# QK-norm attention and SwiGLU block on one core: what the first dummy matmuls read, when the first raw weights are loaded, and a new plan for the weight conversions

## The chip, the cores and the metric

The kernel runs on one core of a Trainium2 chip. The metric is the device time in microseconds (us) of one execution. Each engine works through its own instruction stream in order: PE (TensorE, matmuls), ACT (ScalarE), DVE (VectorE), POOL (GpSimd) and SP (SyncE, here the queue that issues nearly all DMAs). The streams are held together by semaphores only.

## The reference: what is computed

```
q_n, k_n = rmsnorm(q) * g_q, rmsnorm(k) * g_k        # q, k, v: 8 x 12 x 448 x 64
attn     = softmax(q_n @ k_n^T / sqrt(64)) @ v
x        = attn, heads side by side                   # 3584 x 768
out      = (silu(x @ w_gate) * (x @ w_val)) @ w_out   # 768 -> 1536 -> 768
```

`rmsnorm` divides every row of 64 by the root of its mean square plus 1e-6. The weights reach the kernel as 64-bit floats; all else is float32.

## The kernel before, in words

`fast` (line 494) does the work. Two heads of one batch are a pair; there are 48 pairs. Two batches (12 pairs) make a block of the feed-forward part. The kernel first runs attention for pairs 0 to 11, which I call the early phase. Then it alternates: the up products of a block (gate and value, L1467), and the down products of that block (L1650) with the next twelve pairs of attention laid between them. The products use a fast 3x3 matrix scheme with 15 small products. It needs sums and differences ("sides") of weight blocks and of activation blocks, so each raw weight piece is first converted.

**Attention of one pair** (`attention`, L734). SP loads q and k (L759). ACT squares them (L801; POOL does it for pairs 2 and 3, L799) and DVE sums the squares (in two halves for pair 0, L820; in one go for the others, L829). `inverse_root` (L698) then takes the reciprocal root: logarithm and exponential on ACT (L706, L707) and three short steps on DVE (L712 to L714). DVE (pair 0) or POOL (the others) multiplies q and k by the root (L876). PE turns them (L903), DVE drains the turned keys (L911) and ACT the turned queries (L913). After that come the scores (L965), the exponentials on ACT (L980), the row sums (L1074), the weighted values (L1043), and a division on DVE (L1118 to L1144).

**Dummy matmuls** (`warm`, L1739). Their results are used nowhere; they keep PE busy while it has nothing else. Four run at the start on a tile `more` of zeros. Two follow pair 0's root (L716, L717), one of them on the root itself; one has pair 1's keys as its moving operand (L803); one follows pair 0's transposes (L905).

**Converting weights** (`convert`, L1250). There are 24 raw pieces: 16 of the up weights (four for each of four groups g) and 8 of the down weights. Each takes five DMAs on SP (L1266, L1268), two passes on ACT (L1276, L1280), six or nine short steps on DVE (L1297, L1303, L1309), twelve steps on POOL (L1330, L1333) and one store to DRAM on SP (L1358). A piece lies meanwhile in a "place", a stretch of a tile that something else needs later: XS (inside `xs`), HS, ES, GT (inside `gt`), SPARE, PAIRS (inside `work`, which also holds q, k and what is made of them). Piece n+1 of a place waits for the store of piece n. The up products load converted weights on SP (L1422), three loads for each group; a group's loads follow all four of its stores.

**What sets the order.** Nothing is scheduled by hand, and nothing at run time. A planner (`Order`, L365) gets every step with an engine, an estimated duration, a due time (`when`), a rank that moves the due time forward, and the steps that it must follow. It simulates the engines and emits the instructions in the order so found, which becomes fixed for each engine. So a changed due time, rank or dependency can move steps on every queue. The due times of the conversions come from `starts`, `spans` and `counts` (L1766 to L1768): the first seven are planned 9.9 us apart from 7.0 us on; their places come from `turns` (L1765). `MORE` (L668) shifts the planned time of everything from the end of the first block's up products on.

Of the kernel before, what the change touches and what calls it, by code (L numbers as in the profile page):

```python
# [360 lines left out]
def transfer(rows, size):  # L361
    return rows * (6.64 + 0.045 * min(size, 4096)) / 16000.0
# [131 lines left out]
def fast(  # L494
# [41 lines left out]
    nc = tc.nc  # L536
# [3 lines left out]
    P = 128  # L540
# [124 lines left out]
    PRODUCT = 1.504  # L665
    UP, DOWN, BOTH = 30 * NG * PRODUCT, 90.7, 170.0

    MORE = 4.4  # L668

    def block_start(n):  # L670
        return FIRST + n * (UP + BOTH) + MORE * (n > 0)
# [26 lines left out]
    def inverse_root(m, sums, of, when, rank=0.0, tiny=0.0):  # L698


        def estimate():
            ss = of()
            rr = take("rr", m, [P, 2 * NC])[0 : ss.shape[0], 0 : ss.shape[1]]
            tiles["rr", m] = rr
            bias = little[0 : ss.shape[0]] if tiny else 0.0
            nc.scalar.activation(rr, ss, AF.Ln, bias=bias, scale=GAIN**-2)  # L706
            nc.scalar.activation(rr, rr, AF.Exp, scale=-0.5)  # L707

        def improve():
            ss, rr = of(), tiles["rr", m]  # L710
            times = nc.vector.scalar_tensor_tensor
            times(ss, ss, tiny, rr, op0=ALU.add, op1=ALU.mult)  # L712
            times(ss, ss, -0.5 * GAIN**-2, rr, op0=ALU.mult, op1=ALU.mult)
            times(rr, ss, 1.5, rr, op0=ALU.add, op1=ALU.mult)  # L714
            if m == 0:
                warm(rr)  # L716
                warm(more[:, 0])  # L717

        first = order.add(
            "ACT", 0.48, when, estimate, after=[sums], uses=[("ss", m)], takes=[("rr", m)],  # L720
            mode="logarithms", rank=rank,
        )
        return order.add(
            "DVE", 0.63, when + 1.0, improve, after=[first], uses=[("ss", m), ("rr", m)],
            rank=rank, port=True,
        )
# [7 lines left out]
    def attention(m):  # L734
# [19 lines left out]
        def load(x, src):  # L754
            def emit():
                if natural:
                    to = take("qk", (m, x), [R, 2, NJ * D])
                    rows = src[b][2 * c : 2 * c + 2].rearrange("h (p j) d -> p h (j d)", j=NJ)
                    queue.dma_start(to, rows)  # L759
                    return  # L760
                to = take("qk", (m, x), [P, NC, C])
                for g in range(P // C):
                    rows = src[b, 2 * c + g // 2][:, ts(g % 2, C)]
                    queue.dma_start(to[ts(g, C)], rows.rearrange("(c i) f -> i c f", i=C))  # L764


            both = m == 0 and src is k and not natural
            queue = nc.scalar if both else nc.sync
            return add(
                "ACT" if both else "SP", 0.5 if natural else 1.4 if both else 2.4, ready - 28.0, emit, takes=[("qk", (m, x))],  # L770
                moves=[transfer(2 * R, 4 * NJ * D)] if natural else [transfer(S, 4 * C)] * (P // C), early=25.0,
                after=[staged.get(PAIRS)],
            )

        natural = m in NATURAL
        loaded = [load(x, src) for x, src in enumerate((q, k))]

        def load_values():
            x = take("v", m, [P, NJ, 2, D])
# [12 lines left out]
        def square(x):  # L792
            if x == 0:
                take("t", m, [R, 2, 2 * NJ * D] if natural else [P, 2, NC, C])
            of = tiles["qk", (m, x)]
            if natural:
                of = of.rearrange("p h f -> p (h f)")
            if m in SQUARED:
                nc.gpsimd.tensor_tensor(out=tiles["t", m][:, x], in0=of, in1=of, op=ALU.mult)  # L799
            else:  # L800
                nc.scalar.activation(tiles["t", m][:, x], of, AF.Square)  # L801
            if m == 1 and x == 1:
                warm(of[:, 0:S])  # L803

        squares = []
        for x in range(2):
            squares.append(
                add(
                    "POOL" if m in SQUARED else "ACT", 1.04 if m in SQUARED else 0.63 if natural else 0.58,
                    ready - 18.0, lambda x=x: square(x), port=m in SQUARED,  # L810
                    after=[loaded[x], *squares], uses=[("qk", (m, x))] + [("t", m)] * x,
                    takes=[("t", m)] * (1 - x),
                )
            )
# [35 lines left out]
            )  # L850

        sums = None
        for x in range(2 if m == 0 else 0):
            sums = add(
                "DVE", 0.65, ready - 17.0, lambda x=x: summed_half(x), after=[squares[x], sums],
                uses=[("t", m)] + [("ss", m)] * x, takes=[("ss", m)] * (1 - x),
            )
        sums = sums or add(
            "DVE", 1.45 if natural else 1.08, ready - 17.0, summed,
            after=[*squares, clusters.get("turned") if m == 1 else None], uses=[("t", m)], takes=[("ss", m)]  # L860
        )
        if not natural:
            sums = add("ACT", 0.88, ready - 16.0, swap, after=[sums], uses=[("ss", m)])
# [34 lines left out]
        def turn(x):  # L898
            if x:
                take("st", (m, "turned"), [P, 2, TB])  # L900
            turned = tiles["st", (m, "turned")][:, x]
            for j in range(NJ):
                nc.tensor.transpose(turned[:, ts(j, R)], tiles["t", m][:, x, ts(j, P)], ident[0:R, 0:R])  # L903
            if m == 0 and x == 0:
                warm(more[:, 0, 0:Q])  # L905

        def drain(x):
            turned = tiles["st", (m, "turned")][:, x, 0:S].rearrange("p (j r) -> p r j", j=NJ)
# [258 lines left out]
        )  # L1167
        if b % 2 and c % 3 == 2:
            if early:
                first_sides.append((c // 3, when + 6.0, when + 6.0 - 16.0))  # L1170
            else:
                sides(b // 2, c // 3, when + 6.0)

# [11 lines left out]
    def sides(n, c, when, soon=None):  # L1185
# [7 lines left out]
        for i, one, two, op in (  # L1193
# [15 lines left out]
            if n == 0:  # L1209
# [4 lines left out]
                order.add(  # L1214
                    "DVE", 0.62, soon if soon is not None and i in (6, 8, 1, 10, 13, 9) else when,
                    lambda to=x[i], one=x[one], two=x[two], op=op: combined(to, one, two, op),
                    after=[*done[one], *done[two], *free], port=True, rank=55.0 * (n == 0),
                )
            ]
        for i in SLOT:  # L1220
# [28 lines left out]

    def convert(key, src, sums, to, when, place, by_bank):  # L1250

        rank = 0.0 if by_bank else 5.0

        def add(*what, **more):
            return order.add(*what, **dict(rank=rank, **more))
# [6 lines left out]
        def load():  # L1262
# [5 lines left out]
                nc.sync.dma_start(to[:, i], src(k, n))  # L1268

        loaded = add(  # L1270
            "SP", 2.5, when - 12.0, load, after=[staged.get(place), *wait], moves=[transfer(P * n, 8 * P) for n in (2, 2, 3, 1, 1)], early=3.0
        )
        bits = dst.bitcast(U32)
        one = add(
# [158 lines left out]
    def block(n):  # L1433
# [127 lines left out]
        def up_load(g, piece):  # L1561
# [3 lines left out]
                lambda: load_sides(key, up_sides[g], UP_ORDER[5 * piece :][:5], UP_SUMS),  # L1565
                after=[*last_load, *(weights["up", 4 * g + i] for i in range(4))], takes=[key],
                moves=[transfer(4 * P, 4 * P * i) for i in groups(UP_ORDER[5 * piece :][:5], UP_SUMS)],
                early=8.0,
            )
            last_load[:] = [load]  # L1570
            return key, load
# [164 lines left out]

    def warm(of):  # L1739
        rows, n = of.shape  # L1740
        nc.tensor.matmul(banks[0][:, 0:n], more[0:rows, 0, 0:P], of, start=True, stop=True)

    nc.vector.memset(more[:, 0], 0.0)
    for _ in range(4):
        warm(more[:, 0])
    load_tables()
    order.mode["ACT"] = "logarithms"
    for t, x in ((gq2, g_q), (gk2, g_k)):
# [13 lines left out]
    for m in range(EARLY):  # L1762
        attention(m)
    first = [(up_weights, i) for i in range(4 * NG)] + [(down_weights, i) for i in range(2 * NG)]
    turns = [(XS[0], XS[1], HS, SPARE, GT[1], GT[0], HS, SPARE, GT[1],), (SPARE, PAIRS, HS, GT[2], ES,), (PAIRS, SPARE, ES, HS,)]  # L1765
    starts = [LEAD - 3.4, FIRST - 40.1, FIRST + 78.2]  # L1766
    spans = [9.9, 8.3, 9.9]
    counts = [7, 9, 8]  # L1768
    todo = iter(first)
    for n in range(3):  # L1770
# [77 lines left out]
```

## Time and profile before

| | us |
|---|---|
| runs without profile | 1456.33, 1459.54, 1459.80 (median 1459.54) |
| the profiled execution: its own time | 1457.2 |
| its span, first to last instruction | 1455.4 |
| PE busy in the span | 1424.7 |
| first score matmul (L965) starts | 15.20 |
| first exponential of a pair (L980) starts | 16.66 |
| first up product (L1467) starts | 125.14 |

The table is read from the left end of the run: PE has work in almost every microsecond from the first score matmul on, so the time is mostly PE's fixed work, plus the head (until the scores of pair 0 can start), plus short waits, plus the last stores. Times inside the run are counted from the start of the span.

### The profile page before, as it was taken

What the parts mean: (1) busy time and instruction counts of PE and PEld (TensorE: products, weight loads), DVE (VectorE), ACT (ScalarE), POOL (GpSimd) and SP (SyncE); (2) the same over time, 40 slices, a digit from 0 to 9 for tenths busy, and PEclk for the clock granted to TensorE, in tenths of its full rate; (3) what the DMA queues carried; (4) which work ended last, traced back from release to release, by engine and by line L of the source; (5) the groups of instructions that cost most, each with busy time, mean ns of one, the idle gap of its engine ahead of it and who ended that gap; (6) DMA issues with size and microseconds to landing.
All of it is one profiled execution on the core that took longest, in us unless ns stands there. A gap on an engine that the chain in (4) does not pass through costs nothing.

```text
span 1455.4 us, 19339 instructions
## 1 busy us (share of the span) xinstructions
PE 1424.7 (98%) x6736; PEld 689.5 (47%) x6736; DVE 880.6 (61%) x1484; ACT 601.8 (41%) x1210; POOL 401.0 (28%) x476
## 2 busy tenths in 40 slices
PE   8999999999999999999999999999999999999997
PEld 4454455534444555544444455544444445555553
DVE  5888877888766334546877642356676644442533
ACT  6874534476652222365554122255655322212100
POOL 3766656634443000022343100012434300000000
PEclk9999999999999999999999999999999999999999
DMA  8777988854543432542543623354364452323235
GB/s 228 213 219 252 352 280 303 238 152 95 120 107 78 115 109 72 138 107 64 122 103 81 138 73 108 85 132 99 78 127 83 88 134 73 108 73 101 62 102 104
DMA packets 410417, 193.30 MB, mean 133 GB/s; under 512 B 280004, under 2 KB 390852, under 8 KB 410308
## 3 DMA queue, kind: packets, MB, share of 16 engines
q1 hardware_dynamic: 399040, 190.57, 48.7%
q10 hardware_dynamic: 11140, 1.38, 0.7%
q8 instruction: 55, 0.90, 0.3%
q14 instruction: 54, 0.44, 0.1%
q0 software_dynamic: 128, 0.00, 0.0%
HBM read 157.29 MB, written 34.60 MB: 132 GB/s over the span
## 4 chain that ended last, share of the span: by engine, by line
PE 90%; DMA 4%; ACT 2%; DVE 2%; SPq 1%; issue 1%; POOL 0%; DVEq 0%; ACTq 0%; POOLq 0%
PE at L1467 24%; PE mm L1467 24%; PE mm L1650 24%; PE at L1043 8%; PE st L965 7%; PE st L1074 1%; ACT es L980 1%; DMA xs<-in_moe_w_gate_dram 1%; DMA out_dram<-spare 1%; PE mm L1074 1%; SPq L764 0%; DMA work<-in_k_dram 0%; PE st L903 0%; DMA hs<-in_moe_w_val_dram 0%; DMA work<-in_q_dram 0%
## 5 line engine op out<-in xcount | busy, mean ns | idle before, releaser
L1467 PE MATMUL at<-xs,ws 128*128 128x448 f32 x960 | 401.5, 541 | 3.4 <-DVE v L1409 1.0
L1467 PE MATMUL mm<-xs,ws 128*128 128x448 f32 x960 | 400.2, 539 | 0.0
L1467 PEld LDWEIGHTS at<-xs,ws 128*128 128x128 f32 x960 | 181.2, 190 | 186.0 <-issue 165.8
L1467 PEld LDWEIGHTS mm<-xs,ws 128*128 128x128 f32 x960 | 182.1, 190 | 179.4 <-issue 177.9
L883 POOL TENSOR_TENSOR work<-work,rr 128x448 f32<-128x448 f32 x72 | 67.2, 953 | 487.3 <-DVE rr L714 385.8
L1650 PE MATMUL mm<-gt,ws 128*128 128x448 f32 x448 | 175.5, 543 | 0.0
L965 PE MATMUL st<-work 64*64 64x448 f32 (+1 forms) x1536 | 151.0, 500 | 11.8 <-ACT work L913 4.6
L1405 DVE TENSOR_TENSOR gt<-gt,mm 128x448 f32<-128x448 f32 x64 | 39.7, 621 | 189.0 <-PE mm L1467 186.1
L980 ACT ACTIVATE es<-st 128x896 f32<-128x896 f32 x129 | 113.8, 915 | 95.8 <-PE at L1043 82.8
L1650 PE MATMUL mm<-hs,ws 128*128 128x448 f32 x384 | 151.0, 544 | 0.0
L1650 PEld LDWEIGHTS mm<-gt,ws 128*128 128x128 f32 x448 | 83.6, 190 | 83.4 <-issue 80.4
L985 POOL TENSOR_TENSOR sums<-es 128x896 f32<-128x896 f32 x36 | 76.7, 2129 | 163.9 <-PE st L1074 118.8
L1544 ACT ACTIVATE st<-gt 128x448 f32<-128x448 f32 x96 | 52.5, 547 | 161.3 <-DVE gt L1409 85.2
L1403 ACT COPY gt<-mm 128x448 f32<-128x448 f32 x80 | 42.6, 532 | 165.3 <-PE mm L1467 165.1
L1043 PE MATMUL at<-es,v 64*64 64x448 f32 (+1 forms) x1032 | 106.0, 507 | 0.0
L1650 PEld LDWEIGHTS mm<-hs,ws 128*128 128x128 f32 x384 | 71.4, 190 | 71.5 <-issue 70.4
L965 PEld LDWEIGHTS st<-work 64*64 64x64 f32 x1536 | 50.7, 132 | 80.1 <-issue 35.2
L1403 ACT COPY v<-at 128x448 f32<-128x448 f32 x96 | 51.0, 531 | 80.0 <-PE at L1467 80.0
L985 POOL TENSOR_TENSOR sums<-sums,es 128x896 f32<-128x896 f32 x36 | 75.4, 2095 | 2.8
L1043 PEld LDWEIGHTS at<-es,v 64*64 64x64 f32 (+1 forms) x1032 | 44.1, 134 | 56.2 <-issue 48.6
L801 ACT ACTIVATE work<-work 128x448 f32<-128x448 f32 (+1 forms) x92 | 52.5, 585 | 28.9 <-DMA work<-in_k_dram 14.0
L1547 DVE SCALAR_TENSOR_TENSOR gt<-st,v 128x448 f32<-128x448 f32 x96 | 59.7, 623 | 7.7 <-DVE v L1407 0.5
(168 smaller groups left out, 1540.7 us busy)
## 6 DMA issues: line engine op xcount, KB each, us to landing
ws<-up_sides SPq DMA_DIRECT2D x32, 1024.0 KB, 5.5
ws<-down_sides SPq DMA_DIRECT2D x16, 1024.0 KB, 5.6
ws<-down_sides SPq DMA_DIRECT2D x28, 512.0 KB, 4.4
ws<-up_sides SPq DMA_DIRECT2D x16, 768.0 KB, 4.8
out_dram<-spare SPq DMA_DIRECT2D x168, 56.0 KB, 2.1
v<-in_v_dram SPq DMA_DIRECT2D x96, 96.0 KB, 2.5
ws<-up_sides SPq DMA_DIRECT2D x32, 256.0 KB, 6.0
ws<-up_sides SPq DMA_DIRECT2D x16, 512.0 KB, 5.7
```

The costliest lines, as they stand in the source:

```text
L801: nc.scalar.activation(tiles["t", m][:, x], of, AF.Square)
L883: nc.gpsimd.tensor_tensor(out=tiles["t", m][:, x], in0=tiles["qk", (m, x)], in1=rr.to_broadcast([P, NC, C]), op=ALU.mult,)
L965: nc.tensor.matmul(st[ds(D * x, D), h, 0:n], tiles["KT", m][rows, ds(P * j + D * of_keys, D)], tiles["QT", m][rows, ds(Q * of_queries, n)] ...
L980: nc.scalar.activation(e, tiles["st", (m, j)][:, :, 0 : S * width(j) // P], AF.Exp)
L985: nc.gpsimd.tensor_tensor(out=to, in0=tiles["e", (m, 0)] if j == 1 else to, in1=e, op=ALU.add)
L1043: nc.tensor.matmul(tiles["at", (m, x)][ds(D * h, D), ds(0, Q) if early else queries], tiles["v", m][rows, j, h], tiles["e", (m, j)][rows, ...
L1403: nc.scalar.copy(to, ps)
L1405: nc.vector.tensor_tensor(out=to, in0=old, in1=ps, op=ALU.add)
L1467: nc.tensor.matmul(ps(), w[:, which, c, at], xs[:, SLOT[x], c], start=fresh and c == 0, stop=c == NC2 - 1, skip_group_check=True,)
L1544: nc.scalar.activation(take(*act, [P, 2, TB])[:, 0, 0:S], to, AF.Silu)
L1547: nc.vector.scalar_tensor_tensor(to, tiles[act][:, 0, 0:S], 1.0 / SCALE, tiles[ready], op0=ALU.mult, op1=ALU.mult,)
L1650: nc.tensor.matmul(banks[s][:, 0:S], w[:, s, g, at], where[x][:, g], start=fresh and g == 0, stop=g == NG - 1, skip_group_check=True,)
```

## The change

It has six parts. (1) The dummies: the four at the start read zeros that now lie in the first conversion's place (`zeros`, inside `xs`) instead of `more`. A fifth, with pair 1's keys as the moving operand and zeros as the stationary one, is placed right after the load of pair 1's keys, so the first load of raw weights into that place has to follow it. The later dummies use the identity and pair 1's keys. (2) Each conversion's load must follow pair 1's key load in the plan. (3) Pair 1's squares must follow pair 0's logarithm and exponential on ACT. (4) Pair 1's sums of squares come in two halves as pair 0's do, the second after pair 0's keys are drained. (5) The plan: `MORE` from 4.4 to -0.4, conversion rank 5 to 0, the rank of the first block's side sums 55 to 60 with some of them due 2.8 us later, the first seven conversions from 3.1 us later on and 14.0 apart instead of 9.9, and other places for the later ones. (6) A rank of 0 is named for the loads of the up weights, which is what they had.

```
-    MORE = 4.4
+    MORE = -0.4
+    SIDES_RANK = 0.0
...
             if m == 0:
-                warm(rr)
-                warm(more[:, 0])
+                warm(ident, rr)
+                warm(ident, tiles["qk", (1, 1)].rearrange("p h f -> p (h f)"))
...
+        clusters.setdefault("estimate", first)
...
                     queue.dma_start(to, rows)
+                    if m == 1 and src is k:
+                        warm(zeros, to.rearrange("p h f -> p (h f)")[:, 0:S])
...
-            if m == 1 and x == 1:
-                warm(of[:, 0:S])
...
-                    after=[loaded[x], *squares], uses=[("qk", (m, x))] + [("t", m)] * x,
+                    after=[loaded[x], *squares, clusters.get("estimate") if m == 1 else None], uses=[("qk", (m, x))] + [("t", m)] * x,
...
-        for x in range(2 if m == 0 else 0):
+        for x in range(2 if m < 2 else 0):
             sums = add(
-                "DVE", 0.65, ready - 17.0, lambda x=x: summed_half(x), after=[squares[x], sums],
+                "DVE", 0.65, ready - 17.0, lambda x=x: summed_half(x),
+                after=[squares[x], sums, clusters.get("turned") if x else None],
...
-            after=[*squares, clusters.get("turned") if m == 1 else None], uses=[("t", m)], takes=[("ss", m)]
+            after=squares, uses=[("t", m)], takes=[("ss", m)]
...
-                warm(more[:, 0, 0:Q])
+                warm(ident, tiles["qk", (1, 1)].rearrange("p h f -> p (h f)")[:, 0:Q])
...
-                first_sides.append((c // 3, when + 6.0, when + 6.0 - 16.0))
+                first_sides.append((c // 3, when + 6.0, when + 6.0 - 13.2))
...
-                    after=[*done[one], *done[two], *free], port=True, rank=55.0 * (n == 0),
+                    after=[*done[one], *done[two], *free], port=True, rank=60.0 * (n == 0),
...
-        rank = 0.0 if by_bank else 5.0
+        rank = 0.0 if by_bank else 0.0
...
-            "SP", 2.5, when - 12.0, load, after=[staged.get(place), *wait], moves=...
+            "SP", 2.5, when - 12.0, load, after=[staged.get(place), *wait, clusters["loaded"]], moves=...
...
-    def warm(of):
+    zeros = places[XS[0]][:, 0:S]
+
+    def warm(by, of):
         rows, n = of.shape
-        nc.tensor.matmul(banks[0][:, 0:n], more[0:rows, 0, 0:P], of, start=True, stop=True)
-
-    nc.vector.memset(more[:, 0], 0.0)
+        nc.tensor.matmul(banks[0][:, 0:n], by[0:rows, 0:P], of, start=True, stop=True)
+
+    nc.vector.memset(zeros, 0.0)
     for _ in range(4):
-        warm(more[:, 0])
+        warm(zeros, zeros)
...
-    turns = [(XS[0], XS[1], HS, SPARE, GT[1], GT[0], HS, SPARE, GT[1],), (SPARE, PAIRS, HS, GT[2], ES,), (PAIRS, SPARE, ES, HS,)]
-    starts = [LEAD - 3.4, FIRST - 40.1, FIRST + 78.2]
-    spans = [9.9, 8.3, 9.9]
+    turns = [(XS[0], XS[1], HS, SPARE, GT[1], GT[0], HS, SPARE, GT[1],), (PAIRS, HS, GT[2], ES, SPARE,), (PAIRS, SPARE, ES, HS,)]
+    starts = [LEAD - 0.3, FIRST - 40.1, FIRST + 78.2]
+    spans = [14.0, 8.3, 10.0]
```

## The prediction

> **What bounds the kernel now.** I read the page's busy rows first, then the list of what PE waits for, then the order of time in the first 15 us, then one-microsecond windows of the same stretch.
>
> ```profile
> span 1455.4 us, 19339 instructions
> PE 1424.7 (98%) x6736; PEld 689.5 (47%) x6736; DVE 880.6 (61%) x1484; ACT 601.8 (41%) x1210; POOL 401.0 (28%) x476
> ```
>
> PE is the bound, and 30.7 us of the span are all that it does not work. Nothing here shortens PE's real work, so only these can be won.
>
> ```profile
> PE st L965 <- ACT work L913: 4.6, 9, 1.0
> PE mm L1741 <- DVE rr L714: 3.7, 1, 3.7
> ```
>
> The longest single wait of PE's list is a dummy's, for pair 0's root: PE had nothing real to do. The real loss is what delays the first scores (15.20), since PE is nearly full afterwards. In order of time:
>
> ```profile
> 3.79 1.27 ACT L801 ACTIVATE work<-work 112x512 f32<-112x512 f32 x2 [0.91 <-DMA work<-in_q_dram]
> 5.12 0.67 DVE L820 TENSOR_REDUCE ss<-work 112x8 f32<-112x512 f32 x1
> 8.12 0.63 ACT L801 ACTIVATE work<-work 112x512 f32<-112x512 f32 x1 [3.06 <-DMA work<-in_q_dram]
> 8.66 0.29 ACT L706 ACTIVATE rr<-ss,little 112x16 f32<-112x16 f32 x1
> 9.49 0.63 ACT L801 ACTIVATE work<-work 112x512 f32<-112x512 f32 x1 [0.29 <-DMA work<-in_k_dram]
> 9.86 1.29 DVE L876 TENSOR_TENSOR work<-work,rr 112x512 f32<-112x512 f32 x2
> 10.96 1.30 PE L1741 MATMUL mm<-work,more 112*128 112x448 f32 x2
> 12.05 1.70 PE L903 MATMUL st<-ident,work 112*128 112x112 f32 x8
> 14.51 0.63 ACT L913 ACTIVATE work<-st,gg 128x448 f32<-128x448 f32 x1 [4.39 <-DVE work L911]
> 15.04 1.27 ACT L1276 ACTIVATE xs<-xs 128x1152 f32<-128x1152 f32 x1
> ```
>
> Pair 0's sums are ready at 5.79, but the logarithm (L706) stands behind the square of pair 1's q, which waits 3.06 us for its DMA. That costs the root 2.83 us (8.66 against 5.83). Then the windows (PE busy, its loads, DVE, ACT, POOL, granted clock, DMA share, GB/s):
>
> ```profile
> 10.00:11.00 1.00, 1.00 (x5) 0.63 (x6) 1.00 (x2) 0.12 (x1) 0.60 (x1) 1.00 1.09 286
> 11.00:12.00 1.00, 1.00 (x3) 0.35 (x2) 0.15 (x1) 0.00 (x0) 0.00 (x0) 0.68 0.61 146
> 12.00:13.00 1.00, 1.00 (x7) 0.94 (x6) 0.00 (x0) 0.00 (x0) 0.00 (x0) 0.50 0.72 207
> ```
>
> The granted clock is 0.50 while pair 0 is turned: eight transposes take 1.70 us there and 0.96 at 19.35.
>
> **The change, part by part.** *Root before squares.* Sums at 5.79, logarithm and exponential 0.54, root on DVE 0.60 (9.23 to 9.83), both scalings 1.29: q is scaled at 8.32 instead of 11.15. Gain on this chain 2.83 us; from here the PE queue decides.
>
> *The new dummy.* PE's stream is now: four dummies (to 6.21), the dummy on pair 1's keys, one on the root, one of 512 columns, the transposes. So pair 0's transposes, which need nothing of pair 1, stand behind the landing of pair 1's keys, and so do the drains, scores and exponentials of pair 0. This is the wait that the change adds. Its price is the landing. Issued at 2.20, the keys landed at 9.49 before. Two ends: pair 0's keys, issued at 1.20, were squared at 4.42, that is 3.2 us; by that row pair 1's land at 5.4. The Trainium skill ("DMA: Bandwidth & Descriptors", Queues, rings and completion order) says that each DMA engine takes one queue's descriptors in ring order. By that rule raw weights, issued from 2.70 on behind the keys, never delayed them, holding them back wins nothing, and the keys land at 9.5 again. The trace is between: only 95 and 105 GB/s moved from 4 to 6 us, with the weights already queued, so something other than bandwidth held pair 1 there; from 6 on 252 to 351 GB/s moved, and the last packets of pair 1 shared that with weights. The nearest row is that same landing, so I stay near it: 8.3.
>
> From 8.3: keys' dummy 0.75 (two starts 0.38 apart, as at 4.54 and 4.92), root's dummy 0.24, 512 columns 0.87 (0.38 x 512/448, twice), transposes 0.96: 11.1. Drain of keys 0.62, of queries from 11.85 to 12.5 (gg's last product ends at 10.60, so it does not hold this), scores at 12.55: 2.65 earlier. With a landing at 5.4 the transposes start at 8.3, but the query drain waits for gg at 10.6: scores at 11.35, 3.85 earlier. At 9.5: 1.45 earlier.
>
> *The clock.* PE now pauses from 6.21 to 8.3, 2.1 us instead of 3.67. The skill ("TensorE: Matmul & The Clock Gate", Part 1) has a window of about 3.4 us that runs free, and half rate after an idle one; its advice is no pause above about 3 us. By that the clock holds, and I sum with full rate. The row is harsher: the clock fell at about 11.3, when PE had worked 1.5 of the last 3.4 us. If a pause of 2.1 us with unlucky windows is enough, the 512 columns and the transposes cost 0.87 + 0.74 = 1.6 us more.
>
> *Raw weights later.* The first ACT pass on them (15.04, 1.27 us) stood ahead of pair 1's logarithm; in the new ACT order it follows three exponentials. Pair 1's logarithm then follows the query drain directly, its second half sum (0.67) lies beside that drain, and the first exponential starts at 13.1 instead of 16.66. PE's second batch of scores, which waited 0.68 us for it (17.24), no longer waits: 0.6 more. That pass is only moved: by pair 5 ACT has done six passes instead of five, 1.3 us more, and ACT is 96% busy from 25 to 35. What pays for it is idle time: ACT waited 0.99 us for q of pair 5 (36.88), because weights and the read of `fits` (30.2) stood ahead on SP. Now `fits` comes before the first weights and three q/k loads come ahead of the fourth piece's. PE lost 1.42 us from 35 to 45; of the two waits for late exponentials, 0.82 and 0.20 there, I take 0.8.
>
> *The new plan after that.* From 45 to 125 PE is 94% busy and waits mostly for query drains (0.3 to 1.0 each), which stay: nothing. Loads and stores trade places on SP and POOL, with the same number of passes done at the same pair, so I cost that at nothing; the cover is that first weights for the products (issued 99.5) are wanted at 125.1. In blocks 1 and 2 one product moves between the scores of the block's first pair, where PE waited 0.28 + 0.20 and, just before, 0.85 us (642 to 651); I take 0.35 for each block, 0.7; none is possible, and minus 1, since q/k loads now stand before weight loads on SP. Dummies by identity, split sums (0.13 us more DVE work), ranks: nothing; they lie beside PE's wait for the keys.
>
> Sum: 2.65 + 0.6 + 0.8 + 0.7 = 4.75. The profiled execution took 1457.2, so 1452.4 for it; the three runs' median is 2.3 above it. I forecast the median: 1459.54 - 4.75 = 1454.8. A measurement here tells about 0.3%, 4.4 us, from no change, so this is barely outside.
>
> **Rivals.** *The keys land late and the clock falls.* Against it: less traffic beside them. For it: the ring rule, and the 4 to 6 us dip, which came before weights moved. Head 1.45 less 1.6 for the clock, then 0.6 + 0.8 + 0.7: 1.95 gained, 1457.6; with one of the two, 3 to 3.5 gained. Chance 0.36, within 0.3%.
>
> *The weights of the second up group come too late (slower).* Piece 7 moves from SPARE (loaded 96.84) to PAIRS, where a load waits for the early phase's scores (issued 121.0 before, stored 148.2). The group's first load (159.93) already stands on SP behind a store waiting for POOL (154.97) and five DMAs; PE reaches that group at 170, with 10 us for issue and landing (5.5 median). If the conversions keep their old times while PE comes 4.75 earlier, about 5 are left: all slack gone. Each further microsecond is lost whole. One POOL conversion (6.4, 141.74 to 148.2) plus one SP load (4.5) late is 11: 6 us slower than now, 1465; it decides from about 5 us on. Against it: before, four pieces' POOL work lay ahead of that load in nearly the same order. Chance 0.09.
>
> *The keys land by 6 and SP's stalls all go*: 3.85 + 0.6 + 1.4 + 1.5 = 7.3 gained, 1452.2; chance 0.07. The forecast itself has 0.48.
>
> **How the numbers follow.** Faster is forecast plus early keys, 0.55; same 0.36; slower 0.09. The range leaves out most of the slow case and the end of the lucky one: 1450.5 to 1459.0.
>
> **What would show it.** Right: L706 near 5.8; keys' dummy at about 8.3; transposes in 0.96 us at clock 1.00; first scores near 12.5; first up product near 121. Wrong: the keys' dummy at 9.5, a clock of 0.50 from 9 to 13, an up product near 165 waiting for a DMA, or a head that is shorter while the wait returns before 125.

## The result, and the profile after

Eighteen runs of each kernel on one chip: 1455.62 us median after the change (1453.50 to 1458.57), 1457.88 before (1455.58 to 1461.09). The ratio is 0.9984, interval 0.9976 to 0.9992: 2.3 us gained, 1.2 to 3.5 by the interval, where 4.75 was forecast. The time lies in the stated range. About half of the gain did not come, and it was not lost where the rivals put it. The kernel after was timed in this one series, the experiments below in four others.

The page's first rows, then the longest lines of what PE waits for (engine, tile and line waited for; us in total, times, longest):

```profile
span 1452.5 us, 19359 instructions
PE 1424.2 (98%) x6736; PEld 689.4 (47%) x6736; DVE 881.2 (61%) x1485; ACT 603.1 (42%) x1210; POOL 400.7 (28%) x476
```

```profile
PE st L970 <- ACT work L918: 4.7, 10, 1.0
PE at L1472 <- DVE v L1412: 4.0, 2, 3.0
PE st L970 <- ACT work L925: 2.6, 1, 2.6
...
PE st L908 <- POOL work L881: 1.2, 2, 0.9
PE st L970 <- ACT gt L985: 1.2, 1, 1.2
```

The head's dummy wait of 3.7 us is gone. In its place stand a wait of 3.0 us for a product sum on DVE (the longest of this kind before was 1.0) and, in the early pairs, one of 1.2 for ACT and two on POOL that make 1.2 together. The head in order of time:

```profile
5.56 0.31 ACT L707 ACTIVATE rr<-ss,little 112x16 f32<-112x16 f32 x1 [0.84 <-DVE ss L824]
6.78 1.29 DVE L881 TENSOR_TENSOR work<-work,rr 112x512 f32<-112x512 f32 x2
7.54 1.02 PE L1748 MATMUL mm<-work,xs 112*128 112x448 f32 x2
9.47 0.93 PE L908 MATMUL st<-ident,work 112*128 112x112 f32 x8
11.16 0.63 ACT L918 ACTIVATE work<-st,gg 128x448 f32<-128x448 f32 x1 [3.01 <-DVE work L916]
11.85 3.38 PE L970 MATMUL st<-work 64*64 64x224 f32 x32 [1.05 <-ACT work L918]
```

The logarithm no longer waits for pair 1, the keys' dummy starts at 7.54, the transposes take 0.93 us at full clock, and scores start at 11.85: 3.35 us earlier than before. From there on the lead of after over before is read at the same instruction of both profiled executions, at places where PE has the same work behind it in both (the drains of pairs 3 and 4 stand elsewhere in PE's order and are left out):

| at | before | after | lead | forecast |
|---|---|---|---|---|
| first scores | 15.20 | 11.85 | 3.35 | 2.65 |
| key drain of pair 1 | 20.34 | 16.23 | 4.11 | 3.25 |
| key drain of pair 2 | 26.67 | 23.91 | 2.76 | |
| key drain of pair 5 | 52.52 | 51.23 | 1.29 | 4.05 |
| first up product | 125.14 | 123.41 | 1.73 | 4.05 |
| first query drain of block 0 | 295.26 | 294.30 | 0.96 | 4.05 |
| 11th down product of block 0 | 326.08 | 326.90 | -0.82 | 4.05 |
| second query drain after block 1's start | 670.55 | 669.56 | 0.99 | 4.40 |
| PE's last end | 1446.55 | 1445.08 | 1.47 | 4.75 |
| span | 1455.41 | 1452.51 | 2.90 | |

The lead is lost in two places, between 16 and 50 us and at block 0's first pair (295 to 326). The last 1.43 us of the span's difference are no part of the change: from PE's last end to the end of the span the kernel before took 8.86 us in this one execution, and all thirteen other profiled executions, among them one with the old head, took 7.4 to 7.5.

### The profile page after: what moved, and what is told of

Its sections match the earlier page's. It is cut to its first block, busy times and chain, and to the rows that moved or that the text cites. A ratio compares the mean times of both kernels' runs of the same rounds, so it can differ in the third digit from the quotient of the medians.

```text
span 1452.5 us, 19359 instructions
## 1 busy us (share of the span) xinstructions
PE 1424.2 (98%) x6736; PEld 689.4 (47%) x6736; DVE 881.2 (61%) x1485; ACT 603.1 (42%) x1210; POOL 400.7 (28%) x476
## 4 chain that ended last, share of the span: by engine, by line
PE 92%; DVE 2%; ACT 2%; DMA 2%; issue 1%; POOL 1%; SPq 0%; DVEq 0%; ACTq 0%; POOLq 0%
PE at L1472 25%; PE mm L1472 24%; PE mm L1655 24%; PE st L970 8%; PE at L1048 8%; PE st L1079 1%; PE mm L1079 1%; DMA out_dram<-spare 1%; PE st L908 1%; PE mm L1748 1%; ACT es L985 1%; DMA work<-in_q_dram 0%; DVE work L916 0%; SPq L768 0%; ACT work L918 0%
## 5 line engine op out<-in xcount | busy, mean ns | idle before, releaser
L1410 DVE TENSOR_TENSOR v<-v,at 128x448 f32<-128x448 f32 x64 | 39.8, 621 | 40.3 <-PE at L1472 39.8
```

The costliest lines, as they stand in the source:

```text
L1410: nc.vector.tensor_tensor(out=to, in0=old, in1=ps, op=ALU.add)
```

## The experiments

Theory after seeing this: (1) the gate, that is the raw weights' wait for the dummy on pair 1's keys, leaves the DMA engines idle, and the loads of the next pairs pay for it; (2) MORE's new value puts two DVE additions beside POOL's sums at block 0's first pair. Rivals: ACT's conversions take the lead back whatever lands when; the keys' early landing is owed to the gate; the head is worth what it shows and the plan loses it. All ratios below are to the kernel before, on the chip of that run. "First scores", "first up" and "PE's last end" are times in us from the one profiled execution of each kernel.

| kernel | ratio (interval) | first scores | first up | PE's last end |
|---|---|---|---|---|
| after | 0.9984 (0.9976 to 0.9992) | 11.85 | 123.41 | 1445.08 |
| no gate | 0.9968 (0.9955 to 0.9980) | 11.57 | 120.77 | 1445.79 |
| pair 2 ahead of weights | 0.9975 (0.9967 to 0.9984) | 11.93 | 123.00 | 1446.47 |
| gains late | 0.9972 (0.9961 to 0.9982) | 11.64 | 123.02 | 1446.57 |
| squares first | 0.9979 (0.9971 to 0.9988) | 12.15 | 123.22 | 1446.71 |
| block 0's MORE 4.4 | 0.9959 (0.9944 to 0.9974) | 12.06 | 125.38 | 1445.14 |
| MORE 4.4 | 0.9971 (0.9961 to 0.9981) | 11.95 | 123.05 | 1445.48 |
| no gate, block 0's MORE 4.4 | 0.9948 (0.9933 to 0.9962) | 12.09 | 121.53 | 1441.38 |
| the same with a bridge | 0.9942 (0.9929 to 0.9954) | 11.76 | 120.94 | 1441.50 |
| the bridge, with the gate | 0.9958 (0.9944 to 0.9972) | 11.88 | 122.47 | 1442.97 |
| new head, old plan | 1.0037 (1.0022 to 1.0051) | 12.26 | 127.96 | 1453.67 |
| old head, new plan | 1.0001 (0.9993 to 1.0009) | 14.77 | 127.69 | 1447.31 |
| weights ahead of values | 0.9978 (0.9968 to 0.9987) | 15.06 | 124.24 | 1447.92 |

Two limits hold for this table. Between series a difference of 0.001 says little: "gains late" has the rows of after but for POOL's small loads, and 0.9972 in its series where after has 0.9984 in another. So ratios are best compared within one series: no gate, pair 2 ahead, gains late and squares first; the two with MORE 4.4, both together and the new head with the old plan; the bridge, the old head and weights ahead of values. The bridge with the gate was alone in its series. And first scores scatter: five kernels with the same rows up to there (after, the two with MORE 4.4, the bridge with the gate, the new head with the old plan) started them at 11.85 to 12.26.

### The gate

**No gate.** The zeros lie in `more` again, so the first raw weights wait for nothing; no row of PE, ACT or POOL moves (on SP the read of `fits` falls behind three pieces of weights).

```diff
-    zeros = places[XS[0]][:, 0:S]
+    zeros = more[:, 0]
```

> After, with the zeros in the first exponentials' buffer instead of the first conversion's place, so nothing gates the first raw weights; they follow values 0 in SP's queue (about 5.3 us instead of 8.59). Theory A, the gate empties the DMA engines from 7.5 to 9.8 us and pair 2 pays for it: keys of pair 1 still land near 7.5 (within 0.4), the first raw piece lands near 12.5 instead of 16.42, pair 2's queries near 15 instead of 17.39, the PE waits of 1.20 (22.26 us) and 0.94 (27.01) lose at least 1.2 together, and the time is 0.3 to 1.2 us under after's. Theory B, the gate is what makes pair 1 land early: its keys land at 8.5 to 9.5, scores start 1 to 2 us later, and the time is equal to after's or up to 2 us above it.

Theory A held up to 125 us. Three stretches of the kernel after (columns: busy us and count of PE, its loads, DVE, ACT, POOL; granted clock; DMA share; GB/s), then the same three without the gate:

```profile
6.00:7.50 1.50, 1.50 (x3) 0.33 (x1) 1.25 (x5) 0.75 (x2) 0.19 (x1) 1.00 0.88 151
7.50:10.00 2.50, 2.50 (x13) 1.56 (x13) 1.17 (x2) 0.63 (x2) 0.19 (x1) 1.00 0.10 19
10.00:12.00 2.00, 0.95 (x11) 0.60 (x12) 1.22 (x2) 0.84 (x2) 0.00 (x0) 1.00 0.91 295
```

```profile
6.00:7.50 1.50, 1.02 (x4) 0.30 (x3) 0.93 (x4) 1.29 (x4) 0.19 (x1) 1.00 1.14 232
7.50:10.00 2.50, 2.50 (x15) 1.60 (x15) 1.49 (x3) 0.38 (x1) 0.45 (x1) 1.00 1.01 313
10.00:12.00 2.00, 0.95 (x12) 0.54 (x14) 1.22 (x2) 1.06 (x3) 0.00 (x0) 1.00 1.07 312
```

With the gate the DMA engines are busy 0.10 of the time from 7.5 to 10 us, without it 1.01: 735 KB (294 GB/s times 2.5 us) that have to be moved later. From 10 to 20 us the DMA engines have no such pause left in either kernel (243 to 346 GB/s in every 2 us), so what comes behind in the queue stays late. Who pays is seen in POOL's rows, its square of pair 2's queries, of after and then without the gate:

```profile
17.53 2.04 POOL L805 TENSOR_TENSOR work<-work 112x512 f32<-112x512 f32 x2 [2.47 <-DMA work<-in_q_dram]
```

```profile
12.73 2.04 POOL L881 TENSOR_TENSOR work<-work,rr 112x512 f32<-112x512 f32 x2 [4.29 <-ACT rr L708]
14.74 2.04 POOL L805 TENSOR_TENSOR work<-work 112x512 f32<-112x512 f32 x2
```

Pair 2's queries land at 12.97 instead of 17.39, the square follows POOL's scaling at once, and PE's wait of 1.20 at 22.26 is gone. The keys of pair 1 landed at 7.22, no later than with the gate (7.49). The first up product is 2.64 us earlier. Other executions agree: with the gate it starts at 122.47 to 123.41 (six kernels, leaving out the old plan and an execution with a half clock before it), without the gate and with values ahead of weights at 120.77 to 121.53 (three). PE's last end is even 0.71 us later than after's in this execution; the cause comes below. The runs do not tell the gate's cost on their own: 0.9968 stands beside 0.9972 to 0.9979 for the three kernels with the gate in this series, and the intervals overlap.

**Pair 2 ahead of the weights.** With the gate, the issue of the first raw weights is put behind pair 2's two loads; no other row moves.

```diff
-            for i, n, rows in ((0, 2, (1, 3, 0)), (2, 2, (0, 2, 2)), (5, 3, (0, 3, 1))):
...
+            held.append(issue)
...
+                    if m == 2 and src is k:
+                        held.pop()()
```

> After, with the two loads of pair 2 ahead of the first raw weights on SP, and no other row moved on any engine. Theory A (pair 2's landing holds back what the head won): its queries land at 12 to 13 instead of 17.39, POOL squares them right behind its scaling at 15.1 instead of 17.53, pair 2's logarithm is at about 18.5 instead of 20.85, PE's waits of 1.20 and 0.94 us shrink by 1.2 or more, and pair 2's key drain is at about 22.5 instead of 23.91; at the end 0.3 to 1.2 us under after. Theory B (ACT's work from 12 to 45 us sets the pace and the landing only shows): the drain of pair 2 moves, the first up product stays within 0.3 us of 126.5, the time that of after.

Pair 2 landed as A expected (12.73 for its keys), and the wait of 1.20 went. But the first up product moved by 0.4 us only, from 123.41 (the 126.5 of this expectation, and of the one for squares first, is not the first up product of after):

```profile
23.53 2.04 POOL L807 TENSOR_TENSOR work<-work 112x512 f32<-112x512 f32 x2 [2.06 <-DMA work<-in_q_dram]
25.53 1.04 POOL L883 TENSOR_TENSOR work<-work,rr 112x512 f32<-112x512 f32 x1
```

Now POOL waits for pair 3's landing (keys at 24.00, hardly earlier than in after, 24.48; 21.07 without the gate). Its squares stand on POOL ahead of pair 2's second scaling (25.53), and PE waits 1.8 us for that one (0.94 in after). What the gate takes is transfer time, and another order on the queue only chooses who goes short. So neither A nor B was right for this kernel: the loss moved one pair on, and it wasn't ACT that took it.

**Weights ahead of values.** No gate, and values 0 behind the first raw weights, which then stand right behind pair 1's keys as before the change; no other row moves. The edit is the same deferral, for the loads of values 0, taken up behind the first raw weights, with the zeros in `more`:

```diff
+            if m == 0:
+                held.append(issue)
...
+            if place == XS[0]:
+                held.pop()()
```

> After without the gate, and with the first raw weights ahead of values 0 on SP, so that their five loads stand right behind pair 1's keys (from 2.7 us, as before the change) instead of at 5.2 to 7.6; no other row moves. Theory A (transfers issued behind the keys take turns with them): keys of pair 1 land at 8.6 to 9.6 instead of 7.2 to 7.5, PE waits for them 1.5 to 2.5 us more, first scores at 13 to 14 instead of 11.6, and half of that or less is left at the first up product (120.8 without the gate alone). Theory B (keys are held by something of their own, and order on the ring protects them): keys within 0.4 of 7.3, first scores within 0.4 of 11.6.

Theory A for the landing: keys at 9.03, and scores at 15.06. By then 1571 KB had moved (174 GB/s times 9.03 us), where the four loads of pairs 0 and 1 are 917 KB (4 x 112 x 2,048 bytes): over 600 KB from behind them went first. Without the gate and with values next, 1206 KB had moved at the landing (167 times 7.22). So the gate is not needed for an early landing of pair 1: with values ahead of weights the keys landed at 7.22 to 7.90 in all eleven profiled executions, three of them without the gate. That the weights right behind them make them late is less certain: with that order they landed at 9.46 (the kernel before), 9.03 (here) and 7.93 (the old head with the new plan, where 376 KB, 163 GB/s times 7.93 us less those 917, had gone first). What sets how much goes first was not found. PE waited 2.1 us for these keys, and its clock halved right behind:

```profile
6.15:9.56 3.41, 1.35 (x5) 0.45 (x4) 2.50 (x6) 1.61 (x4) 0.69 (x1) 1.00 0.99 285
9.56:12.97 3.41, 3.41 (x10) 1.86 (x9) 0.00 (x0) 0.12 (x1) 0.19 (x1) 0.50 0.98 250
```

That part of the expectation was wrong which said that half of the shift or less would be left: all 3.5 us were still there at the first up product (124.24 against 120.77); 1.8 of them are the landing, 1.7 the half clock. Without the gate the head was worth its full length up to there. With the gate it was not: after starts its scores 3.21 us before this kernel and its first up product only 0.83 before it.

**Gains late, squares first.** Two single steps of the head. In the first, POOL's four small loads go behind its memsets; in the second, the logarithm of pair 0 loses its place ahead of pair 1's squares.

```diff
-    for t, x in ((gq2, g_q), (gk2, g_k)):
...
     make_identity(nc, ident)
+    for t, x in ((gq2, g_q), (gk2, g_k)):
...
```

```diff
-                    after=[loaded[x], *squares, clusters.get("estimate") if m == 1 else None], ...
+                    after=[loaded[x], *squares], ...
```

> After, with POOL's four small loads of the gains issued behind its memsets and the identity, from about 2.6 us instead of 1.27. Theory A (the small loads cause the dip of 143 KB from 4 to 5 us): the dip moves or goes, the keys of pair 1 land at 6.3 to 7.0 instead of 7.49, first scores up to 0.6 us earlier than 11.85. Theory B (the dip is the large loads' own): keys within 0.3 of 7.49. Either way the gains land near 9 and the query drain, 11.16 now, does not wait for them; the time is within 0.7 us of after's.

> After, with pair 1's query square again ahead of pair 0's logarithm on ACT. The square waits for queries at 6.87, so the logarithm starts at 7.5 instead of 5.56, the root ends at 8.7 instead of 6.75, transposes begin at about 11.4 and first scores at 13.8 instead of 11.85. Theory A (pair 2's landing, not the head, sets the pace from 20 us on): of these 2 us, less than 0.7 are left at the first up product (126.5) and at the end. Theory B (a shorter head shortens the kernel): 1.5 to 2 us longer than after, with the whole shift still there at 126 us. If PE's pause of over 3 us (6.8 to 11) halves its clock in the head, 1 us more at the scores.

The small loads are not what slows the DMA from 4 to 5 us: 147 GB/s against 143, keys at 7.29. What does was not found. The order of root and squares, 2.83 us of the forecast's chain, is worth 0.3 us at most, which is within the scatter of first scores, and nothing at the first up product (123.22): with queries landing at 6.60 the square ends at 7.2 and the root at 8.5, and the transposes, which stand behind the dummy on the keys in any case, start at 9.77 instead of 9.47. The expectation of 11.4 had put the whole delay of the old landing on it.

### Block 0's first pair

**MORE for block 0's pairs alone, and everywhere.** The due times of block 0's pairs get the old 4.4 (first run), or all blocks do (second).

```diff
-        return block_start(n) + UP + MORE * (n == 0)
+        return block_start(n) + UP + 4.4 * (n == 0)
```

> After, with MORE back at 4.4 in the due times of block 0's pairs alone (blocks 1 and 2 keep -0.4): no PE row moves; on DVE the two side sums of block 0's first pair stand ahead of the product sum w again, as before. Theory A (that order puts two DVE additions beside POOL's sums, 2.43 and 2.49 us instead of 0.62, and PE pays): PE's wait at 302.94 falls from 2.98 to about 0.9, everything from 306 us on is 1.6 to 2.0 earlier than in after, and the time is 1.5 to 3 us under after's, the more as the wait of 2.98 no longer halves PE's clock in some executions. Theory B (the long additions have slack): PE's wait stays above 2.5 and the time that of after.

> After, with MORE at 4.4 everywhere as before the change. Theory A: block 0 gains 1.6 to 2.0 us as in the run with block 0's due times alone, blocks 1 and 2 lose what they won (waits of 0.28 + 0.20 at each first pair return, 0.85 at 642 perhaps): 0.9 to 1.8 lost, so 0 to 1 us under after's time. Theory B (MORE's new value is worth its change): 1 to 2 us longer than after.

DVE's rows of after, then POOL's beside them, then DVE's, POOL's and PE's wait with block 0's old due times:

```profile
300.50 2.43 DVE L1188 TENSOR_TENSOR hs<-gt,hs 128x448 f32<-128x448 f32 x1
302.85 2.49 DVE L1526 TENSOR_TENSOR gt<-gt,w 128x448 f32<-128x448 f32 x1
305.26 0.61 DVE L1412 TENSOR_TENSOR v<-v,at 128x448 f32<-128x448 f32 x1
```

```profile
300.05 2.39 POOL L990 TENSOR_TENSOR sums<-es 128x896 f32<-128x896 f32 x1 [2.07 <-ACT es L985]
302.52 2.34 POOL L990 TENSOR_TENSOR sums<-sums,es 128x896 f32<-128x896 f32 x1
```

```profile
301.66 0.62 DVE L1188 TENSOR_TENSOR hs<-gt,hs 128x448 f32<-128x448 f32 x1
302.20 0.61 DVE L1412 TENSOR_TENSOR w<-w,mm 128x448 f32<-128x448 f32 x1
302.85 2.42 DVE L1526 TENSOR_TENSOR gt<-gt,w 128x448 f32<-128x448 f32 x1
```

```profile
302.66 2.12 POOL L990 TENSOR_TENSOR sums<-es 128x896 f32<-128x896 f32 x1 [2.71 <-ACT es L985]
304.86 2.36 POOL L990 TENSOR_TENSOR sums<-sums,es 128x896 f32<-128x896 f32 x1
```

```profile
PE at L1472 <- DVE v L1412: 0.9, 1, 0.9
```

An addition of 0.62 us takes 2.42 to 2.49 when POOL starts one of its sums up to 0.45 us ahead of it, and ends 0.5 us after that sum. (The Trainium skill, "SBUF — State Buffer", Who interferes with whom, says that a DVE instruction with two SBUF inputs contends with a POOL instruction that reads SBUF, over ports that the two share under an exclusive lock; these rows agree.) MORE at -0.4 does two things here: it brings w's sum ahead of the two side sums on DVE, and on ACT one exponential of the pair ahead of a square, so that POOL's first sum starts 2.61 us earlier (300.05 against 302.66) where PE runs 2.0 us earlier. Two additions then stand in such places instead of one, and PE waits 2.98 us for v behind them instead of 0.9. Which of the two moves counts for more was not separated. With the old order the stretch from the last up products to block 0's 11th down product (269.63 to 326.90, 57.27 us) takes 55.53: theory A, 1.74. The end of PE is nevertheless that of after, since in this execution PE's clock halved at 29.09, behind a wait of 1.8; the runs have the gain (0.9959 against 0.9984), but from two series, and here of five executions. With MORE at 4.4 everywhere, PE's times stand 1.64 us under this run's at the 11th down product, 0.09 at 985 us, and 0.34 over them at the end: 1.5 us go again in block 1 and 0.4 in block 2. So MORE's new value helps blocks 1 and 2 and hurts block 0. (MORE 4.4 everywhere shows no wait for v, since PE's own clock had halved at 295.93.)

**Both together.** The zeros in `more` and block 0's old due times, as in the two diffs above.

> Zeros in the exponentials' buffer (no gate on the first raw weights) and block 0's due times of before, the rest of after. Theory A (the two are independent, and PE's clock halves for 3.41 us only where PE was idle over about 1.9 us of a 3.41 us window): first up product at 120.8, PE's wait of 2.98 at block 0's first pair falls to 0.9, last product 4.2 to 4.6 us earlier than after's where the 2.56 us wait at 292 halves no clock, 2.5 to 3 where it does; median 3.5 to 5 us under after's. Theory B (the gain of 2.6 us at the first up product is always given back at block 0): last product within 1 us of the run with block 0's due times alone.

Theory A: PE's last end is 3.7 us earlier than in after, with a half clock at 293.74 in the profiled execution, and the ratio is 0.9948 (0.9959 with the gate in the same series). This also answers what became of the 2.64 us that the run without the gate lost on its way. Its windows at block 0's first pair, each 3.41 us long, laid along the edges of the granted clock's changes:

```profile
289.00:292.40 3.40, 0.84 (x7) 0.12 (x5) 2.23 (x4) 2.48 (x8) 1.13 (x2) 1.00 1.05 349
292.40:295.80 3.40, 3.40 (x18) 1.34 (x19) 1.20 (x4) 1.60 (x4) 1.84 (x2) 0.50 0.98 289
302.65:306.06 3.41, 1.13 (x3) 0.68 (x4) 3.41 (x5) 1.62 (x2) 1.22 (x1) 1.00 0.05 13
306.06:309.47 3.41, 3.41 (x6) 1.35 (x4) 2.28 (x4) 2.54 (x4) 0.00 (x0) 0.50 0.21 35
```

Twice PE was busy for about a third of such a window or less (0.84 and 1.13 us), and twice the next window ran at half clock, 1.7 us lost each time. In the profiled execution of after neither happened, though its rows there are the same: its window from 290.73 on still held 1.72 us of work. That this is chance is seen in its eighteen runs: the nine with a mean clock of 0.998 or 0.999 have spans of 1451.7 to 1453.6, the nine at 0.995 to 0.997 have 1454.0 to 1456.7. Where in those runs the clock fell was not recorded; of the other eleven profiled executions with the new head, seven had a half clock from 292 to 297 us on and one from 316, so block 0's first pair is the likely place.

**A bridge.** Sixteen dummies ahead of the scores of block 0's first pair, in the bank that these then overwrite.

```diff
+    BRIDGE = 16
...
+            if m == EARLY and j == 3:
+                for _ in range(BRIDGE):
+                    nc.tensor.matmul(st[:, 0, 0:P], ident, ident, start=True, stop=True)
```

> No gate, block 0's due times of before, and 16 dummies of 128 columns by the identity (some 1.9 us) ahead of the first scores of block 0's first pair, where PE waits 2.56 us for its query drain. Theory A (that wait halves PE's clock for 3.41 us in about six executions of ten): no execution has a half clock near 292, the wait is below 0.9, the mean clock of the executions is 0.997 to 0.999, and the median is 0.3 to 1.2 us under that of the same kernel without dummies (ratio 0.9948 to the kernel before), so ratio 0.994 to 0.9946. Theory B (the dummies delay the scores, or the clock falls elsewhere): ratio 0.995 or more.

```profile
289.82 3.73 PE L968 MATMUL st<-ident 128*128 128x128 f32 x32
293.48 1.36 PE L974 MATMUL st<-work 64*64 64x224 f32 x16
```

All five runs have a mean clock of 0.999, and their spans lie within 1.1 us (1448.3 to 1449.4). The dummies took 3.73 us where 1.9 was reckoned (two passes of 0.117 each), so scores start about 1 us later than their queries allow; ten would take 2.3, which was not tried. The ratio of 0.9942 is the best of all, though not told apart from 0.9948 by the intervals. Nor does the small spread show the bridge's worth: without it the five runs of the same kernel lie within 1.5 us, at clocks of 0.997 to 0.999.

**The gate on top of it.** The same, with the zeros back in the first conversion's place.

> The kernel with block 0's due times of before and the 16 dummies ahead of block 0's first scores, with the change's gate put back (zeros in the first conversion's place); against the same kernel without the gate this is the gate alone, free of half clocks in block 0. Theory A (the gate empties the DMA engines at 7.5 to 9.8 us and pair 2's loads land 4 us later): first up product at 123.2 to 123.6 instead of 120.9, and 2 to 2.8 us longer: ratio to the kernel before 0.9955 to 0.9965 where it was 0.9942. Theory B (a later wait swallows the difference): ratio within 0.0005 of 0.9942.

The gate alone costs 1.5 us in the profiled executions (first up 122.47 against 120.94, PE's last end 1442.97 against 1441.50), neither of which had a half clock before the last microseconds. The ratios differ by 0.0016, on two chips and with overlapping intervals. The 1.5 us are less than A's 2 to 2.8: PE's wait for the exponentials of pair 1 was 0.6 here and 1.2 in after.

### Head and plan apart

The first kernel has after's head and all of the plan's old numbers, the second the old head and the new numbers (`turns`, `rank` and the sides' 13.2 go the same way).

```diff
-    MORE = -0.4
+    MORE = 4.4
...
-    starts = [LEAD - 0.3, FIRST - 40.1, FIRST + 78.2]
-    spans = [14.0, 8.3, 10.0]
+    starts = [LEAD - 3.4, FIRST - 40.1, FIRST + 78.2]
+    spans = [9.9, 8.3, 9.9]
```

> After's head (zeros in the first conversion's place, gate, root ahead of squares, half sums) with all of the plan's numbers as before the change (MORE 4.4, the places' turns, LEAD - 3.4, spans 9.9, 8.3, 9.9, ranks 5 and 55, 16.0). Theory A (the new plan is worth something to this head): first scores at 11.85 as in after, but conversions come due 3 us sooner and push the pairs' work, so the first up product is 0.5 to 2.5 us later than after's 123.4, and the time 0 to 3 us above after's. Theory B (the plan gives back the head's gain): first up product at 121 to 122, time 1 to 2.5 us under after's.

> The kernel before with the plan's new numbers alone (MORE -0.4, the places' turns, LEAD - 0.3, spans 14, 8.3, 10, ranks 0 and 60, 13.2). Theory A (the plan's worth is that conversions no longer hold up the products when the pairs run earlier; with the old head it only moves things): first up product within 1 us of 125.1, blocks 1 and 2 without the waits of 0.28 and 0.20, and the time within 1.5 us of the kernel before. Theory B (the plan carries the gain of the whole change): 2 us or more under the kernel before.

```profile
PE mm L1472 <- DVE hs L1314: 5.5, 1, 5.5
```

With the old plan the new head makes the kernel slower. PE stands 2.8 us ahead of the kernel before at 107 us and then waits 5.5 us at the first up product. That wait is not for weights: their loads were issued from 105.97 to 114.13, and the last landing on record is at 119.91. It is for DVE, which ends a conversion late (127.35 to 127.90). The conversion uses the same bank of PSUM (the memory of matmul results, here `mm`) that the first product writes. The clock halves behind the wait (0.57 on the mean from 124 to 132 us), and again at block 0's first pair, where PE waits 4.4 us. Theory A, though larger than expected: PE's last end is 7.1 us later than before.

The old head with the new plan is the kernel before, to 0.1%. Its first up product is 2.55 us later, more than the 1 us expected, with a half clock at 33.12 on the way. At 640 us it is 3.6 behind, at PE's last end 0.76: the new plan wins back 2.8 us from block 1 on, as it does in after. Neither part gains anything alone. The new head without the gate was not run with the old plan.

## Why the prediction was right in its range, and where it was not

- *The number*: the range of 1450.5 to 1459.0 is wide; it holds the median of the kernel before on this chip too (1457.88). That 1455.62 lies near the forecast 1454.8 is luck: the forecast was taken from 1459.54, and the kernel before was 1.66 us faster on this chip. The gain, 2.3 of 4.75, is the fairer measure.
- *Root before squares, 2.83 us on the chain*: the row moved as said (logarithm at 5.56), but by itself it is worth 0.3 us at most. The gain of the head comes from pair 1's landing, and from the full clock behind it.
- *Keys of pair 1 at 8.3*: landed at 7.49. The end taken was too near to the old row. The ring order by itself would have had 9.5, if later transfers never delay an earlier one. But the sentence of the Trainium skill that the prediction used ("DMA: Bandwidth & Descriptors", Queues, rings and completion order) goes on that a later descriptor may finish its write before an earlier one. In the run with weights next in the queue over 600 KB from behind the keys had moved when they landed, so the reading that they are never delayed does not hold here. With the weights in the same place another execution had the keys at 7.93: the delay is not the same each time.
- *Clock at full rate in the head*: right, in this execution even without a pause, since the dummies ran at half their rate until 7.4 us and ended with the landing. Where PE did wait 2.1 us for keys, the clock halved: the harsher row was the right one to fear, and the advice of the Trainium skill that the prediction weighed, no pause above about 3 us ("TensorE: Matmul & The Clock Gate", Why this matters for your kernels), would not have kept the clock.
- *Head 2.65 and second scores 0.6*: 3.35 and 0.76. Right, and larger.
- *35 to 45 us, 0.8 gained by idle DMA waits*: this step failed. It took the raw weights' later issue for free ("That pass is only moved"). Of 4.11 us, 2.38 were lost from 16.23 to 123.41. The gate leaves the DMA engines idle for 2.25 us (0.90 of 2.5), pair 2 lands 4.4 us later than without it, and 2.64 us come back when it is taken away.
- *The new plan: nothing but 0.7 in blocks 1 and 2*: blocks 1 and 2 gave more (1.81 and 0.65 around their first pairs, 0.36 lost between). Block 0's first pair was not looked at and lost 1.78, by two DVE additions behind POOL's sums. Between 123 and 295 us 0.77 more went, in short waits of the up products; that was not followed up. And the plan is no small thing beside the head: without it PE waits 5.5 us at the first up product, for a bank and not for the weights that the prediction watched.
- *Rivals*: the late keys didn't come, and at the second up group PE waited for no weights. The measured 2.3 is near the first rival's 1.95, within the 0.3% to which 0.36 was given, but by another cause.
- *The clock after the head*: left out of the sum. A half clock of 3.41 us costs 1.7 us and lowers the mean clock of an execution by 0.0012. By the mean clock, about half of after's executions had at least one more than the profiled one. How often the kernel before had them on that chip is not known. On the three chips of the experiments its 84 runs have a median mean clock of 0.996, after's eighteen 0.9975, so that the kernel before may lose one half clock more in each execution. That would be 1.7 us, nearly the size of the whole gain; what share of the 2.3 us is the clock's stays open.

## What to carry to other kernels

Before holding a transfer back, ask what the DMA engines do meanwhile: if the queue is full later on, the idle time comes back as a late landing (2.25 us of it cost 1.5 to 2.6 us of PE here), and with the values next in the queue pair 1 landed as early without the gate. A change of due times has to be read at each place where they act, with the pairs of engines that can't work side by side. When PE waits at the start of a stage, ask for the bank that it writes as well as for the data that it reads. A gap of PE is to be priced with the half clock behind it. Executions are to be compared by their mean clock before a difference of one or two microseconds is read.

## What the runs showed of the hardware

- PE's clock halved for 3.41 us or twice that, behind windows of 3.41 us (laid along the edges of the clock's changes) in which PE had still worked. In the fourteen profiled executions, from the first change on and with the last microseconds left out, all windows at full clock with up to 1.39 us of work were followed by a half clock. Of six with 1.40 to 1.64 us three were (1.46, 1.48, 1.64) and three were not (1.40, 1.47, 1.51). None from 1.68 us up was. Once halved, it stayed so in one case behind a window with 2.14 us of work. PE's busy time is modelled, so the border is not sharp. A wait of 1.8 to 2.6 us is enough when it falls into one window, and the edges lie elsewhere in each execution.
- A kernel's runs spread with the clock: after's eighteen lie within 5.1 us, the faster nine at a mean clock of 0.998 or 0.999.
- Transfers that stand behind others in SP's queue moved 376 and 654 KB before the landing of those ahead of them, within 7.9 and 9.0 us.
- An addition on DVE beside one of POOL's sums took 2.42 to 2.49 us instead of 0.62.
- The dummies of 448 columns at the start run at 0.75 us a pass until the clock's first change, which came at 4.53 us in one execution and at 7.43 in another.
